# The border between an attention layer and its feed-forward layer: residual on TensorE, key sums ahead of the last X products, kv by rows of X, and the first tiles' outputs at other places

## The chip, the cores and the metric

The kernel runs on one core of one Trainium2 chip. The metric is the device time of one execution in microseconds (us). The kernel before took 1200.74, 1198.84 and 1199.76 us in three runs, 1199.76 in the median.

## The reference

Four residual layers over x of 2048 rows by 512 columns in bfloat16, and the gradient of the result with respect to x and all weights:

```python
phi = lambda t: jnp.where(t > 0, t + 1, jnp.exp(t)) + 1e-6
def _A_ref(x, wqkv, wo):                    # 32 heads of 16 columns
    q, k, v = split_heads(x @ wqkv)
    pq, pk = phi(q), phi(k)
    kv = einsum("bhsd,bhse->bhde", pk, v)
    z = einsum("bhsd->bhd", pk)
    o = einsum("bhqd,bhde->bhqe", pq, kv) / (einsum("bhqd,bhd->bhq", pq, z) + 1e-6)
    return merge_heads(o) @ wo
def _B_ref(x, w_gate, w_up, w_down):        # F = 1376
    return (sigmoid(x @ w_gate) * (x @ w_up)) @ w_down
x = x + _A_ref(layernorm(x), wqkv, wo)
x = x + _B_ref(layernorm(x), w_gate, w_up, w_down)
x = x + _A_ref(layernorm(x), wqkv, wo)
x = x + _B_ref(layernorm(x), w_gate, w_up, w_down)
```

The layers are called L0 (attention), L1 (feed-forward), L2 and L3; L0 and L2 share their weights, as L1 and L3 do.

## The kernel before, in words

The 2048 rows are 16 tiles (st = 0 to 15) of 128 rows. The order of each engine's instructions is that of the program text: it is written out by hand, and the engines run ahead of one another as far as the buffers allow. PSUM has eight banks in named pools: "t", "g" and "u" two banks each, "y" and "ln" one each (L144). A tile taken from a pool waits until the pool's oldest one has been read.

**Attention, first part (`kq_fwd`, L556).** For each tile the K and Q projections (L604), phi on ACT and DVE, and the running product X = pk-transposed times h, four accumulators of 128 by 512 in the "g" and "u" banks (L612). The value projection is never formed for every row: kv = X W_v. POOL adds the pk tiles up in `zs`, all but the last two. Then comes the part that the change rewrites, from L734 on: the sum over all rows, z, as products with matrices of ones: ones in float32 times `zs` (L735), then pk 14, the four X products of tile 14, pk 15 (L738); ACT copies z out as `zb` (L744). The four X products of tile 15 follow, each accumulator evacuated by ACT (L750), then kv from the four rows of X with the column block outermost (L758), masked on DVE to `kvbdT` (L760), M = kvbdT times wo (L765) in four banks, and MT (L776), which only the backward part reads. `late_q` does the Q projection of tiles 14 and 15, which was put off (L604 by its line); their `phi` halves finish it on DVE. A Sigmoid table is loaded on ACT (L771), as the feed-forward layer needs it.

**The attention outputs (`attn_fronts`, L805).** For one tile: `prod` is pq times zb on POOL, or on DVE (L815); `front1` sums it by head (DVE); `front2` adds epsilon, takes the reciprocal `rden` and scales pq to `pqn` (DVE, L831 to L833), and every second tile stores; `front3` transposes pqn on PE through the one "ln" bank (L355), and ACT copies it out as pqnT (L364); `attn_mm` is four products of pqnT with M into the "y" bank (L854); `attn_add` adds the old x on DVE (L862) and starts the layernorm statistics `ln.stats`: two DVE instructions (L448, L450) and three on POOL (L451 to L454), which leave `rstd` and `nmr`. `ln.apply` then normalizes on ACT (L459), and `stage_T` transposes h on PE through the "ln" bank, with DVE copying hT out.

**Feed-forward (`ab_fwd`, L892).** For each tile: gate and up products in three column blocks gu0, gu1, gu2 of 512, 512 and 352 columns (L909), two sigmoids on ACT (L911, L913), hh on DVE (L914), a product on POOL (L915), hh transposed in three groups `transposes(T, 0..2)` through the two "t" banks (L923) and copied out by ACT (L926, L928); `finish` is the down product of the tile before, into the "y" bank (L935), with its add on DVE (L937). The attention outputs of tile st + 2 or st + 3 are woven into tile st.

**Fill groups.** The weights' transposes for the backward part are cut into groups of four (some fewer) PE transposes through a "t" bank (L390 in L1, L416 and a like line in L3), with one evacuation on DVE or ACT. There are 16 groups in L1 and 34 in L3. Three are issued in `tail`, between `kq_fwd` and `ab_fwd`, a fourth at the end of tile 0; the rest are shared out by `fill.share(st)`, which is what is left over the tiles that are left: one for each of tiles 4 to 15 in L1, two for each of tiles 1 to 15 in L3. In a tile the first group goes behind gu0 and the others behind `finish` and `front3`, in front of `transposes(T, 2)`.

Of the kernel before, what the change touches and what calls it, by code (L numbers as in the profile page):

```python
# [67 lines left out]
def kernel(  # L68
# [78 lines left out]
    with tc.tile_pool(name="wfwd", bufs=1, reuse_waits="tile") as wfwd, ExitStack() as lctx, tc.manual_schedule(engines=EM):  # L147
# [44 lines left out]
        with tc.tile_pool(name="aq0", bufs=1, reuse_waits="tile") as aq:  # L192
            A = kq_fwd(k, aq, 0, lns[0], lns[1], x_bf)
            with tc.tile_pool(name="wt_stage", bufs=2, reuse_waits="tile") as wt_stage:
                fill = Fill(wT_groups_a(k, wt_stage))
                A.tail(fill)
                ab_fwd(k, A, lns[1], fill, nxt=lns[2])
        xctx.close()
        with tc.tile_pool(name="aq2", bufs=1, reuse_waits="tile") as aq:
# [32 lines left out]
            A.tail(fill)  # L232
# [229 lines left out]
class FwdLN:  # L462
# [9 lines left out]
    def stats(self, st):  # L472
        if st < NST:
            self.nmr[st] = ln_stats(self.k, self.k.xs[st][:], self.rstd(st))
# [13 lines left out]
    def stage_T(self, st):  # L488
        if st >= NST:
            return  # L490
        k = self.k
        h_t = self.hs.pop(st)
        hT = k.lnres["hT"].tile([P, NDC, P], BF16, name="hT")
        transpose_blocks(k, k.ps["ln"], hT[:], [h_t[:, c * P:(c + 1) * P] for c in range(NDC)], "vector", tag="ln_tp")
        self.hTs[st] = hT
# [60 lines left out]
def kq_fwd(k, aq, l, ln, ln_next, x_src=None):  # L556
# [10 lines left out]
    with ExitStack() as ctx:  # L567
# [7 lines left out]
        else:  # L575
            X_sb = big.tile([P, NDC, D], BF16, name="X_sb")
            MT_sb = big.tile([P, NDC, D], BF16, name="MT_sb")
        cnt = [0]
# [155 lines left out]
        z_ps = mm_tile()  # L734
        nc.tensor.matmul(z_ps[:], lhsT=k.ones32[:], rhs=zs, start=True, stop=False)  # L735

        def z_mm(st):
            nc.tensor.matmul(z_ps[:], lhsT=k.ones_sq[:], rhs=pk_all[:, st, :], start=False, stop=(st == NST - 1))  # L738

        for st in range(NST - ZLAG, NST - 1):  # L740
            z_mm(st)
        X_some(NST, NST - 2)
        z_mm(NST - 1)
# [3 lines left out]
        A.front2(0)  # L747
        for ic in range(NDC):
            X_mm(NST - 1, ic)
            nc.scalar.copy(X_sb[:, ic, :], X_ps[ic][:])  # L750
        nc.sync.dma_start(out=sv["X"].rearrange("(c p) j -> p c j", p=P), in_=X_sb[:])

        kv_ps = ps_tile(k, "y", [P, D], F32, "kv_ps")
        kv3 = kv_ps[:].rearrange("p (c f) -> p c f", c=NDC)
        for c in range(NDC):
            cs = slice(c * P, (c + 1) * P)
            for ic in range(NDC):
                nc.tensor.matmul(kv3[:, c, :], lhsT=k.wqkv[:, ic, 2 * D + c * P:2 * D + (c + 1) * P],  # L758
                                 rhs=X_sb[:, ic, cs], start=(ic == 0), stop=(ic == NDC - 1))
        nc.vector.tensor_tensor(kvbdT[:], kv3, k.bdmask[:].unsqueeze(1).to_broadcast([P, NDC, P]), ALU.mult)  # L760
        A.front3(0)
        A.prod(1, nc.vector)
        for c in range(NDC):
            m_ps = ps_tile(k, "gu"[c % 2], [P, D], F32, "M_ps")
            nc.tensor.matmul(m_ps[:], lhsT=kvbdT[:, c, :], rhs=k.wo[:, c, :], start=True, stop=True)  # L765
            evac_copy(k, A.M_sb[:, c, :], m_ps[:], "vector" if c % 2 else "scalar")
        A.front1(1)
        A.attn_y(0)
        A.front2(1)
        phis = [late_q(st) for st in range(NST - QLATE, NST)]  # L770
        nc.scalar.activation(k.tab[:], k.neg[:], ACT.Sigmoid)  # L771
# [6 lines left out]
        A.front3(1)  # L778
        phis[0]()
        A.ln.apply(0)  # L780
        for jc in range(NDC):
            nc.scalar.copy(MT_sb[:, jc, :], mt_ps[jc][:])
        nc.sync.dma_start(out=sv["MT"].rearrange("(c p) j -> p c j", p=P), in_=MT_sb[:])
        A.attn_mm(1)
        phis[1]()
    k.kv[l] = dict(kvbdT=kvbdT, zb=A.zb, rden_all=A.rden_all)

    def tail(fill):
        fill("tt", "vector")
        A.ln.stage_T(0)  # L790
        A.prod(2)
        A.prod(3)
        A.attn_add(1)
        A.front1(2)
        A.front2(2)
        A.extra = fill.mm("t")
    A.tail = tail
# [7 lines left out]
def attn_fronts(k, A, pool, small):  # L805
# [17 lines left out]
    def front2(st):  # L823
# [5 lines left out]
        den = f["den"]  # L829
        f["pqn"] = cur["pqn"][:, st % 2, :]  # L830
        nc.vector.tensor_scalar(den[:], den[:], EPS, None, ALU.add)  # L831
        nc.vector.reciprocal(A.rden_all[:, st, :], den[:])
# [6 lines left out]
    def front3(st):  # L839
        if st >= NST:  # L840
# [4 lines left out]
                         "scalar", tag="ln_tp")  # L845
        f["T"] = pqnT

    def attn_mm(st):
# [3 lines left out]
        y_ps = F_[st]["y"] = ps_tile(k, "y", [P, D], F32, "y_ps")  # L852
        for c in range(NDC):
            nc.tensor.matmul(y_ps[:], lhsT=pqnT[:, c, :], rhs=A.M_sb[:, c, :],  # L854
                             start=(c == 0), stop=(c == NDC - 1))
# [12 lines left out]

    A.attn_mm, A.attn_add = attn_mm, attn_add
    A.prod, A.front1, A.front2, A.front3, A.attn_y = prod, front1, front2, front3, attn_y  # L870


# [19 lines left out]
def ab_fwd(k, A, ln, fill, nxt=None, out_cb=None, last_cb=None):  # L892
# [3 lines left out]
    with ExitStack() as ctx:  # L896
# [53 lines left out]
        for st in range(NST):  # L950
# [5 lines left out]
            nfill = fill.share(st)  # L956
            if st == 0:
                gu(T, hT, 0)
                A.extra("vector")
                A.front1(FLAG)  # L960
                A.front3(2)
# [3 lines left out]
                A.attn_y(2)  # L965
                ln.stage_T(1)
                gu(T, hT, 2)
                A.front2(FLAG)
            else:
                A.prod(st + FLAG)  # L970
                gu(T, hT, 0)
                if st == 1:
                    A.front3(FLAG)
                else:
# [5 lines left out]
                if st == 1:  # L980
                    A.attn_y(FLAG)
# [3 lines left out]
                gu(T, hT, 2)  # L985
                A.front2(st + FLAG)
            if l == 1 and st == NST - 1:
                nc.scalar.activation(k.tab[:], k.neg[:], ACT.Exp)
            transposes(T, 1)
            ln.apply(st + YLAG)  # L990
# [5 lines left out]
            if st == 0:  # L996
                fill("t", "vector")
# [771 lines left out]
```

## Time and profile before

| | |
|---|---|
| three runs | 1200.74, 1198.84, 1199.76 us; median 1199.76 |
| the profiled execution | 1199.19 us |
| its span | 1197.5 us (1.69 lie around it) |
| mean granted TensorE clock | 0.998 |

Busy time of one engine over the span counts its instructions' durations, a matmul's from its start to its last result. Where the share of PE is high, what matters is when it stands still. For that the region of the change is cut into stretches, which are the same for both pairs of layers: from the z sum (L735) to the first gate product of tile 0 (L909), from there to the first of tile 1, and from there to the first product of finish(0) (L935).

| stretch | L0 to L1 (us) | L2 to L3 (us) |
|---|---|---|
| z to tile 0's first gate product | 53.57 to 70.49 | 260.26 to 276.08 |
| to tile 1's | 70.49 to 79.80 | 276.08 to 285.38 |
| to finish(0) | 79.80 to 86.20 | 285.38 to 292.01 |

The column PEclk of a stretch is the clock that the throttle granted: 1.00 is full speed, and it falls to 0.50 in whole windows of 3.41 us.

### The profile page before, as it was taken

What the parts mean: (1) busy time and instruction counts of PE and PEld (TensorE: products, weight loads), DVE (VectorE), ACT (ScalarE), POOL (GpSimd) and SP (SyncE); (2) the same over time, 40 slices, a digit from 0 to 9 for tenths busy, and PEclk for the clock granted to TensorE, in tenths of its full rate; (3) what the DMA queues carried; (4) which work ended last, traced back from release to release, by engine and by line L of the source; (5) the groups of instructions that cost most, each with busy time, mean ns of one, the idle gap of its engine ahead of it and who ended that gap; (6) DMA issues with size and microseconds to landing.
All of it is one profiled execution on the core that took longest, in us unless ns stands there. A gap on an engine that the chain in (4) does not pass through costs nothing.

```text
span 1197.5 us, 21853 instructions
## 1 busy us (share of the span) xinstructions
PE 1175.6 (98%) x8302; PEld 717.0 (60%) x8302; DVE 730.5 (61%) x1414; ACT 593.2 (50%) x1100; POOL 290.2 (24%) x498
## 2 busy tenths in 40 slices
PE   8989999998999999999999999999999999999999
PEld 4445555544555555555556568965556745547888
DVE  7788886777777556665784760056664976761211
ACT  6667776546776754543644651144444635630010
POOL 5646765425666410000110010000100110110000
PEclk9999999999999999999999999999999999999999
DMA  8834455434446777976856859558897685749875
GB/s 269 291 124 164 169 177 186 155 137 166 179 152 220 248 224 249 333 228 208 260 177 200 251 162 314 141 157 260 257 296 223 219 262 169 220 127 338 280 199 163
DMA packets 266233, 256.05 MB, mean 214 GB/s; under 512 B 43280, under 2 KB 251024, under 8 KB 261264
## 3 DMA queue, kind: packets, MB, share of 16 engines
q1 hardware_dynamic: 266128, 254.65, 66.6%
q8 instruction: 65, 1.06, 0.4%
q14 instruction: 40, 0.33, 0.1%
HBM read 135.69 MB, written 118.92 MB: 213 GB/s over the span
## 4 chain that ended last, share of the span: by engine, by line
PE 93%; DVE 4%; ACT 2%; DMA 1%; issue 0%; POOL 0%; DVEq 0%; ACTq 0%
PE p_ps L1412 17%; PE dh_ps L1174 13%; PE dh_ps L1627 7%; PE p_ps L1396 6%; PE dhh_ps L1059 6%; PE u_ps L909 6%; PE g_ps L909 6%; PE y_ps L935 6%; PE T_ps L1134 3%; PE y_ps L854 2%; PE GT_ps L1539 2%; PE dpk_ps L1658 2%; PE dp_ps L1514 2%; PE t_mm L604 2%; PE t_tp L923 2%; PE X_ps L612 2%
## 5 line engine op out<-in xcount | busy, mean ns | idle before, releaser
L1412 PE MATMUL p_ps<-p_set,p_a 128*128 128x256 bf16 (+1 forms) x2032 | 210.3, 264 | 0.4 <-DVE dw_stg L1386 0.4
L1412 PEld LDWEIGHTS <-p_a 128*128 128x128 bf16 x2048 | 186.0, 98 | 22.8 <-issue 0.5
L1067 DVE TENSOR_TENSOR dd<-dhh_ps,ssd 128x512 bf16<-128x512 f32 x144 | 82.5, 629 | 134.3 <-PE dhh_ps L1059 131.3
L1138 ACT COPY ddT<-T_ps 128x1024 bf16<-128x1024 bf16 (+1 forms) x96 | 83.0, 867 | 124.7 <-PE T_ps L1134 124.3
L1033 POOL TENSOR_SCALAR ab<-c 128x2 f32<-128x2 f32 x64 | 12.3, 191 | 435.7 <-DVE junk L1030 421.5
L915 POOL TENSOR_TENSOR ssd_t<-hh_t,oms 128x512 bf16<-128x512 bf16 (+1 forms) x96 | 101.6, 1064 | 55.5 <-ACT out_t L219 41.1
L1174 PEld LDWEIGHTS <-ddT 128*128 128x128 bf16 (+1 forms) x704 | 67.7, 98 | 69.3
L909 PEld LDWEIGHTS <-hT 128*128 128x128 bf16 x768 | 71.1, 98 | 56.6 <-DVE hT L362 1.0
L1386 DVE TENSOR_TENSOR dw_stg<-p_ps,dw_stg 128x512 bf16<-128x512 f32 (+3 forms) x43 | 28.0, 653 | 106.7 <-PE p_ps L1412 84.9
L909 PE MATMUL g_ps<-wg,hT 128*128 128x512 bf16 (+1 forms) x384 | 90.0, 357 | 0.6 <-DVE hT L362 0.6
L909 PE MATMUL u_ps<-wu,hT 128*128 128x512 bf16 (+1 forms) x384 | 90.0, 357 | 0.0
L914 DVE TENSOR_TENSOR hh_t<-u_ps,ssd_t 128x512 bf16<-128x512 f32 (+1 forms) x96 | 61.0, 636 | 45.9 <-PE u_ps L909 24.5
L1174 PE MATMUL dh_ps<-wgT,ddT 128*128 128x512 bf16 (+1 forms) x352 | 86.2, 379 | 0.0
L1059 PE MATMUL dhh_ps<-wdT,gT 128*128 128x512 bf16 x372 | 82.5, 357 | 0.0
L935 PE MATMUL y_ps<-wd,hhT 128*128 128x512 bf16 (+1 forms) x352 | 81.3, 379 | 0.6 <-DVE x L937 0.6
L1174 PE MATMUL dh_ps<-wuT,ddT 128*128 128x512 bf16 (+1 forms) x352 | 81.3, 379 | 0.0
L1396 PE MATMUL p_ps<-p_a,p_set 128*128 128x512 bf16 (+1 forms) x352 | 81.2, 379 | 0.0
L1025 ACT ACTIVATE t_sb<-dh_ps,rstd_all 128x512 f32<-128x512 f32 x64 | 44.0, 687 | 72.1 <-issue 38.4
L1030 DVE SCALAR_TENSOR_TENSOR junk<-t_sb,h_ld 128x512 bf16<-128x512 f32 x64 | 44.0, 687 | 49.3 <-ACT t_sb L1025 48.4
L911 ACT ACTIVATE ssd_t<-g_ps 128x512 bf16<-128x512 f32 (+1 forms) x96 | 53.2, 554 | 30.8 <-PE g_ps L909 30.6
L1388 ACT CAST dw_stg<-p_ps 128x512 bf16<-128x512 f32 (+2 forms) x43 | 24.1, 560 | 65.9 <-PE p_ps L1412 58.9
L1396 PEld LDWEIGHTS <-p_set 128*128 128x128 bf16 (+1 forms) x352 | 33.6, 100 | 34.9
(241 smaller groups left out, 2164.4 us busy)
## 6 DMA issues: line engine op xcount, KB each, us to landing
p_set<-sv_hdd SPq DMA_DIRECT2D x30, 1024.0 KB, 6.0
sv_ssd<-ssd_t SPq DMA_DIRECT2D x32, 688.0 KB, 3.4
ssd<-sv_ssd SPq DMA_DIRECT2D x24, 688.0 KB, 5.1
sv_hdd<-dd SPq DMA_DIRECT2D x48, 320.0 KB, 3.6
sv_hdd<-hh_t SPq DMA_DIRECT2D x32, 320.0 KB, 2.6
h_ld<-sv_h SPq DMA_DIRECT2D x32, 256.0 KB, 4.6
p_a<-sv_h SPq DMA_DIRECT2D x16, 512.0 KB, 6.1
p_set<-sv_dqk SPq DMA_DIRECT2D x8, 1024.0 KB, 7.8
```

The costliest lines, as they stand in the source:

```text
L909: nc.tensor.matmul(ps[:, 0:w], lhsT=hT[:, kc, :], rhs=w_sb[:, kc, c0:c0 + w], start=(kc == 0), stop=(kc == NDC - 1))
L911: nc.scalar.activation(ssd_t[:, 0, c0:c0 + w], g_ps[:, 0:w], ACT.Sigmoid)
L914: nc.vector.tensor_tensor(hh_t[:, c0:c0 + w], u_ps[:, 0:w], ssd_t[:, 0, c0:c0 + w], ALU.mult)
L915: nc.gpsimd.tensor_tensor(ssd_t[:, 1, c0:c0 + w], hh_t[:, c0:c0 + w], oms[:, 0:w], ALU.mult)
L935: nc.tensor.matmul(y_ps[:], lhsT=T["hhT"][0:r, fc, :], rhs=k.wd[0:r, fc, :], start=(fc == 0), stop=(fc == NFC - 1))
L1059: k.nc.tensor.matmul(ps[:, 0:w], lhsT=gT[:, jc, :], rhs=k.wdT[:, jc, c0:c0 + w], start=(jc == 0), stop=(jc == NDC - 1))
L1067: k.nc.vector.tensor_tensor(dd[:, a, c0:c0 + w], ps[:, 0:w], ssd[:, a, c0:c0 + w], ALU.mult)
L1138: nc.scalar.copy(ddT[:, :, f0:f0 + nfull, :], tps[:, :, 0:nfull, :])
L1174: nc.tensor.matmul(T["dh"][:], lhsT=ddT_block(T, a, fc), rhs=(k.wuT, k.wgT)[a][0:r, fc, :], start=(i == 0), stop=(i == 2 * NFC - 1))
L1396: nc.tensor.matmul(ps[0:r, :], lhsT=set_t[:, st, c * P:c * P + r], rhs=self.ops[j["l"], "g"][:, st, :], start=(st == 0), stop=(st == NST - 1))
L1412: nc.tensor.matmul(ps[:, icl * w:(icl + 1) * w], lhsT=self.ops[j["l"], "h"][:, st, ic * P:(ic + 1) * P], rhs=set_t[:, st, 0:w], start=(st ...
L1627: nc.tensor.matmul(dh_ps[:], lhsT=lhsT, rhs=rhs, start=(i == 0), stop=(i == len(ops) - 1))
```

## The change

- z: the ones products for `zs`, pk 14 and pk 15 are issued in a row into the "y" bank, in front of the X products that are left.
- X: the fourth accumulator is evacuated by DVE instead of ACT.
- kv: the row of X is the outer loop and the column block the inner one, in a "t" bank; behind rows 0 and 1 stands one more product each (`on(1)`: identity times pk of tile 0, 128x512, whose result nobody reads). `rden(0)` is split off `front2(0)`, and the latter stands behind the mask.
- Tiles 0 and 1: `attn_res` adds the old x on PE as the first product into the "y" bank, the identity times x: in bfloat16 in L0 (the input x), in float32 in L2 (a float32 identity `eye32`, made on POOL with the pools). `attn_out` then takes the statistics from PSUM, and ACT copies x out of PSUM behind them. `attn_add(1)` is gone from the tail.
- In L0 alone: `on(2)` behind the first residual product and `keep_on()(3)` behind the second, five more such products.
- late_q(14) stands in front of attn_mm(0), late_q(15) behind the MT products; the copies of MT are issued one by one between other ACT work; the pqnT of tile 1 is evacuated by DVE, hT of tile 0 by ACT; the Sigmoid table load comes last.
- `tail` is gone, and so is the fourth group at the end of tile 0: all fill groups fall into `share`, which gives one for each of tiles 1 to 14 and two for tile 15 in L1, two for each of tiles 1 to 11 and three for each of tiles 12 to 15 in L3.
- Tile 0: attn_y(2) moves from in front of gu2 to behind transposes(1), and front3(2) behind gu2. Tile 1: front3(3) stands behind gu1, attn_y(3) behind gu2.

The backward part is untouched. The diff, cut to its core:

```diff
+        if l == 0:
+            eye = k.ident
+        else:
+            eye = big.tile([P, P], F32, name="eye32")
...
-        z_ps = mm_tile()
+        z_ps = ps_tile(k, "y", [P, D], F32, "z_ps")
         nc.tensor.matmul(z_ps[:], lhsT=k.ones32[:], rhs=zs, start=True, stop=False)
+        for st in range(NST - ZLAG, NST):
             nc.tensor.matmul(z_ps[:], lhsT=k.ones_sq[:], rhs=pk_all[:, st, :], start=False, stop=(st == NST - 1))
-        for st in range(NST - ZLAG, NST - 1):
-            z_mm(st)
-        X_some(NST, NST - 2)
-        z_mm(NST - 1)
         nc.scalar.copy(A.zb[:], z_ps[:])
         A.prod(0, nc.vector)
         A.front1(0)
-        A.front2(0)
+        X_some(NST, NST - 2)
         for ic in range(NDC):
             X_mm(NST - 1, ic)
-            nc.scalar.copy(X_sb[:, ic, :], X_ps[ic][:])
+            evac_copy(k, X_sb[:, ic, :], X_ps[ic][:], "vector" if ic == NDC - 1 else "scalar")
+        A.rden(0)
+        on = keep_on()
+        kv_ps = ps_tile(k, "t", [P, D], F32, "kv_ps")
+        for ic in range(NDC):
+            for c in range(NDC):
...
+            if ic < NDC - 2:
+                on(1)
+        nc.vector.tensor_tensor(kvbdT[:], kv3, ...)
+        A.front2(0, False)
+        A.attn_res(0, eye)
+        if l == 0:
+            on(2)
...
         A.front3(0)
+        phis = [late_q(NST - 2)]
+        A.attn_mm(0)
         A.prod(1, nc.vector)
+        A.attn_out(0)
+        A.prod(2)
         A.front1(1)
-        A.attn_y(0)
         A.front2(1)
...
+        mt_copy(0)
+        mt_copy(1)
+        phis.append(late_q(NST - 1))
+        A.ln.apply(0)
+        A.attn_res(1, eye)
+        if l == 0:
+            keep_on()(3)
+        A.front3(1, "vector")
+        mt_copy(2)
+        A.ln.stage_T(0, "scalar")
         phis[0]()
+        A.attn_mm(1)
+        mt_copy(3)
+        A.attn_out(1)
         phis[1]()
+        nc.scalar.activation(k.tab[:], k.neg[:], ACT.Sigmoid)
...
-    def tail(fill):
-        fill("tt", "vector")
-        A.ln.stage_T(0)
-        A.prod(2)
-        A.prod(3)
-        A.attn_add(1)
-        A.front1(2)
-        A.front2(2)
-        A.extra = fill.mm("t")
...
+    def attn_res(st, ident):
+        y_ps = F_[st]["y"] = ps_tile(k, "y", [P, D], F32, "y_ps")
+        nc.tensor.matmul(y_ps[:], lhsT=ident[:], rhs=k.xs[st][:] if A.x_src is None else A.x_src[:, st, :],
+                         start=True, stop=False)
+
+    def attn_out(st):
+        y_ps = F_.pop(st)["y"]
+        A.ln.stats(st, y_ps[:])
+        nc.scalar.copy(k.xs[st][:], y_ps[:])
...
+            A.prod(st + FLAG)
             if st == 0:
+                A.front1(2)
                 gu(T, hT, 0)
-                A.extra("vector")
-                A.front1(FLAG)
-                A.front3(2)
+                A.front2(2)
                 ln.apply(1)
                 gu(T, hT, 1)
                 transposes(T, 0)
-                A.attn_y(2)
                 ln.stage_T(1)
                 gu(T, hT, 2)
-                A.front2(FLAG)
+                A.front3(2)
             else:
-                A.prod(st + FLAG)
                 gu(T, hT, 0)
-                if st == 1:
-                    A.front3(FLAG)
-                else:
+                if st > 1:
                     A.attn_y(st + YLAG)
...
                 gu(T, hT, 1)
                 if st == 1:
-                    A.attn_y(FLAG)
+                    A.front3(FLAG)
                 transposes(T, 0)
                 ln.stage_T(st + 1)
                 A.front1(st + FLAG)
                 gu(T, hT, 2)
+                if st == 1:
+                    A.attn_y(FLAG)
                 A.front2(st + FLAG)
...
             transposes(T, 1)
+            if st == 0:
+                A.attn_y(2)
+                A.front1(FLAG)
+                A.front2(FLAG)
             ln.apply(st + YLAG)
-            if st == 0:
-                fill("t", "vector")
```

## Prediction

> **What bounds the kernel now.** I read the page first: PE's share, then the chain.
>
> ```profile
> span 1197.5 us, 21853 instructions
> ...
> PE 1175.6 (98%) x8302; PEld 717.0 (60%) x8302; DVE 730.5 (61%) x1414; ACT 593.2 (50%) x1100; POOL 290.2 (24%) x498
> ...
> PE 93%; DVE 4%; ACT 2%; DMA 1%; issue 0%; POOL 0%; DVEq 0%; ACTq 0%
> ```
>
> PE is the bound, and the chain leaves it for DVE and ACT 6% of the time. PE work that is moved costs what it cost; only PE's idle time can be won. So I split the region that the diff touches, at both borders (L0 into L1, L2 into L3), into three stages: from the z sum to the first gate product of the first tile (st0), on to that of st1, on to the first product of finish(0). This is the view of busy time by stretches:
>
> ```profile
> core 0: us, PE busy (x) PEld busy (x) DVE busy (x) ACT busy (x) POOL busy (x), PEclk, DMA share, GB/s
> 56.43:59.84 3.41, 2.08 (x22) 1.26 (x20) 2.73 (x6) 2.21 (x6) 0.00 (x0) 1.00 0.46 162
> 59.84:63.26 3.42, 3.06 (x8) 1.14 (x9) 2.46 (x5) 1.59 (x3) 0.00 (x0) 0.50 0.32 111
> 271.47:274.88 3.41, 2.02 (x22) 1.21 (x20) 2.83 (x5) 3.38 (x7) 3.07 (x4) 1.00 0.43 150
> 53.57:70.49 16.92, 13.44 (x89) 6.89 (x88) 12.72 (x27) 10.01 (x18) 3.43 (x5) 0.90 0.40 142
> 260.26:276.08 15.82, 12.30 (x88) 6.41 (x87) 12.09 (x26) 9.85 (x18) 3.43 (x5) 1.00 0.33 114
> 276.08:285.38 9.30, 7.15 (x51) 3.96 (x52) 7.85 (x18) 5.38 (x11) 4.15 (x7) 1.00 0.18 63
> 285.38:292.01 6.63, 6.63 (x51) 3.86 (x50) 4.58 (x10) 4.97 (x11) 5.00 (x5) 1.00 0.70 234
> ```
>
> A stage's busy PE counts each matmul's latency. By issue pitch (bf16 128x512 0.216 us, 128x352 0.149, 128x128 0.056; f32 128x512 0.86, the two records of the ones32 row, .43 apart, being one product) L2's stages hold 10.40, 6.79 and 6.63 us of work, so 5.42, 2.51 and 0 us of idle. L0's later stages read 9.31 and 6.40. L0's first is 1.10 longer than L2's: in 59.84 to 63.26 the granted clock is 0.50 and eight 512-wide products stand 0.42 apart. In the window ahead, PE's starts fill 0.37 of the time.
>
> **Step 1, z to g_ps.** The sums of the last two pk tiles move in front of eight X products: zb starts at 261.8 instead of 262.6. The X copies were four on ACT (2.06 us, paced by ACT); the fourth now goes to DVE. With kv by rows of X, three rows run as their copies land and only the last waits: kv ends 1.02 earlier, and so do kvbdT and M (266.88 to 265.86). Added on PE: L2 two f32 identity products (1.72) and two fillers (0.43); L0 two bf16 ones and seven fillers (1.94). The f32 product was never run here as an identity: bound 0.22 (bf16 row) to 0.86 (ones32 row), taken 0.86, the same type and shape. The first lies under the wait for kvbdT (264.9 to 265.8); uncovered, either costs 0.86.
>
> late_q(14)'s four products (0.86) now stand in the wait for M's copies, their exp on ACT behind two of these. On POOL, L2's two instructions for eye32 come with the pools at the head of the layer, some 40 us ahead of their use (its first projections are at 219.1), and on SP the MT store goes behind attn_mm(1); nothing in the forward pass reads it.
>
> Then y(0) at 267.9, BN 269.0 (from PSUM, unseen: between 0.42, a DVE copy out of PSUM, and 0.81, ACT's apply of this shape; taken 0.69, its own row from SBUF below), apply at 271.3. Transposes of pqn(1) start at 271.86; stage_T(0) needs the one "ln" bank, which DVE's evacuation (0.39) frees at 272.76; hT(0) goes by ACT (0.58): 272.76 + 0.17 + 0.26 + 0.58 + 0.07 = 273.85 is the new g_ps. Stage: 13.59 against 15.82. Its work is 10.40 + 2.15 − 0.67 (three fill groups gone, step 4) = 11.9, so its idle falls from 5.42 to 1.7.
>
> **Step 2, st0.** ACT has the x copy of tile 1 (0.58; up to 0.81 by the apply row) and the Sigmoid table load (1.28 in its row) in front of sig0, now 276.5. PE waits 0.64 for hh, 0.27 at stage_T(1), 0.35 at front3(2), and 0.62 for pqnT(2). attn_y(2) runs at 281.27, behind transposes(1) instead of in front of gu2. Next g_ps: 282.30. Stage 8.45 against 9.30: 6.79 − 0.22 (one group gone) of work and 1.88 of idle.
>
> **Step 3, st1: what attn_y(2)'s new place costs.** The trace has the same chain, under other work:
>
> ```profile
> 281.71 1.03 PE L854 MATMUL y_ps<-M_sb,pqnT 128*128 128x512 bf16 x4
> ...
> 282.77 0.69 DVE L862 TENSOR_TENSOR x<-y_ps,x 128x512 f32<-128x512 f32 x1 [0.31 <-PE y_ps L854]
> ...
> 283.50 0.69 DVE L448 BATCH_NORM_STATS2 ln_stats<-x 128x6 f32<-128x512 f32 x1
> ...
> 284.23 0.18 DVE L450 BATCH_NORM_AGGREGATE ln_mv<-ln_stats 128x2 f32<-128x6 f32 x1
> ...
> 285.48 0.27 POOL L454 TENSOR_SCALAR ln_nmr<-ln_mv,rstd_all 128x1 f32<-128x1 f32 x1
> ...
> 285.78 0.81 ACT L459 ACTIVATE hstage<-x,ln_nmr,rstd_all 128x512 bf16<-128x512 f32 x1 [0.78 <-POOL ln_nmr L454]
> ...
> 286.90 0.59 ACT L911 ACTIVATE ssd_t<-g_ps 128x512 bf16<-128x512 f32 x1
> ```
>
> From the add to the apply it is 3.0 us, and the apply stands in ACT's queue in front of the hhT copies and the next sig0. After: y(2)'s last product 281.9, add 282.3, apply 285.35. ACT stands 3.66, and sig0, whose g_ps is ready at 283.2, comes at 286.5; hh 287.1, t_tp(0) 287.88. PE idles 1.67 there, 1.05 at stage_T(2) (the "ln" bank waits for pqnT(3)'s copy behind them on ACT) and 0.73 at finish(0) (the "y" bank waits for tile 3's add). Stage 10.08 against 6.63.
>
> L2: 13.59 + 8.45 + 10.08 = 32.12 against 31.75, **+0.37**. L0 at full clock likewise 32.12 against 32.63: **−0.51**. At each border a wait of 0.38 in st2 (front3(4) behind pqnstage; 89.12 in L0) goes with the shift: **−0.75**.
>
> **Step 4, the fill groups.** Four transposes cost 0.22. Four per border lay in idle time; all now fall into the full loop: in L1 three are paid (0.67), in L3 four (0.89). L1's last tile gets two, its 512 KB store then standing in SP's queue in front of the next layer's hT: 0.27, bounds 0 to 1.7. L3's tiles 12 to 15 get three instead of two. The "t" ring has two banks, taken in the order fill1, t0, t1, fill2, fill3, t2: t2's transposes wait for fill2's evacuation, on DVE behind finish's add or on ACT. The trace has such a ring wait at the old tail:
>
> ```profile
> 274.52 0.61 PE L416 MATMUL wT_ps<-ident,wd 128*128 128x128 bf16 x8
> ...
> 274.94 0.76 DVE L362 COPY wdT<-wT_ps 128x512 bf16<-128x512 bf16 x2 [0.57 <-PE wT_ps L416]
> ...
> 275.42 0.32 PE L416 MATMUL wT_ps<-ident,wd 128*128 128x128 bf16 x3
> ```
>
> The eight were issued by 274.96, the next at 275.42: 0.46 idle. With the add in front I get 0.65, 0.62, 0.87, 0.62: **+2.76**.
>
> **Step 5, the clock.** Step 3's waits (1.67, 0.22 of work, 1.05) make a 3.41 us stretch with PE's share down to 0.20, and one that starts anywhere within about 2.0 of 3.41 us falls below 0.43, the share that kept full clock from 271.47; 0.37 lost it. So each border probably has one half-clock window. Price: 1.1 (L0's row) to 1.7 (half of 3.41), taken 1.4. One, **+1.4**; L0's old one is already left out above.
>
> The Trainium skill, "TensorE: Matmul & The Clock Gate", section "Why this matters for your kernels", asks for no PE-idle gap above about 3 us, one such window bringing half clock; by it 1.67 is harmless, which is rival B. Here the window at half clock followed gaps of 0.46 us at most, so the trace disagrees. The page's section "A second HAM failure mode: psum-queue depth-cycling", frequent micro-idles, is what the trace shows.
>
> **Sum** on the profiled execution, 1199.19 (span 1197.5 and 1.69 around it; 0.57 below the median 1199.76): −0.51 + 0.37 − 0.75 + 0.67 + 0.89 + 0.27 + 2.76 = +3.70, 1202.9; with one slow window **1204.3**. With two 1205.7, up to 1206.3 at 1.7 each.
>
> **Rivals.**
> - **A, forecast, 0.56**: own range 1202.9 to 1206.3.
> - **B, full clock at both borders, 0.16**: 1202.9. For it: 271.47 held at 0.43. Against: 0.37 did not, and 0.20 is lower.
> - **C, third fills hidden, 0.09**: where ACT takes the extra evacuations (every other tile) they land in time, half of 2.76 goes, and the clock holds too: 1204.3 − 1.38 − 1.4 = 1201.5. For: ACT is 50% busy. Against: 0.46 at the tail though DVE came at once.
> - **D, the other side, 0.12**: step 3's chain doesn't hold PE. sig0 would have to run as soon as g_ps is ready (283.2), so that nmr(2) follows y(2) by under 1.2 us instead of 3.4; then both borders lose 3.45 of idle and the slow window goes: 1204.3 − 6.9 − 1.4 = 1196.0. For: before has the chain and no idle at all in that stage. Against: the 3.0 us above, and ACT's order.
> - **E, the fillers don't do what they say, 0.07**: L0 keeps its slow window: 1204.3 + 1.1 = 1205.4.
>
> Two in ten left out are D and the ends of A: **1201.0 to 1206.5**; the unknown f32, BN and copy costs (each under 0.9, partly covered) lie within it. A measurement tells some 0.2%, 2.4 us, from no change (1197.4 to 1202.2): faster is D, 0.12; C and the low end of B, 0.12, are the same; slower 0.76.
>
> **What would show it.** Right: M 1.0 earlier after z; stages near 13.6, 8.45, 10.1; ACT idle over 3 us ahead of apply(2); t2's transposes waiting in L3's tiles 12 to 15; a granted clock of 0.5 just behind st1's start. Wrong: stage 3 near 6.6 (D), clock 1.00 throughout (B), no idle in those four tiles (C), 0.5 within L0's first stage (E). The forecast fails most easily on step 3, which gives 6.9 of the sum's terms, and on the clock, whose windows shift from run to run.

## The result and the profile after

The changed kernel takes 1206.11 us in the median (1205.15 to 1207.33, 6 runs), the kernel before, on the same chip, 1200.05 (1198.84 to 1200.74, 6 runs): a ratio of 1.0051, 95% interval 1.0039 to 1.0064. It is slower by some 6 us, inside the range of 1201.0 to 1206.5 and 1.8 above the forecast of 1204.3. The profiled execution took 1206.06 with a span of 1204.3.

The page of the changed kernel, its span, its busy times and the chain by engine:

```profile
span 1204.3 us, 21892 instructions
...
PE 1179.6 (98%) x8317; PEld 718.6 (60%) x8317; DVE 728.1 (60%) x1409; ACT 595.4 (49%) x1105; POOL 291.7 (24%) x500
...
PE 64%; DMA 1%; DVE 0%; ACT 0%; issue 0%; DVEq 0%
```

PE is busy 4.0 us longer, about what the added products take by issue pitch (1.94 in L0 and 2.15 in L2), and the rest of the 6.8 us of span is PE standing still. (The chain names PE 64% here: it was followed back less far, which says nothing of the time.) The busy time by stretches, cut at the same marks as before, L0 first, then L2:

```profile
core 0: us, PE busy (x) PEld busy (x) DVE busy (x) ACT busy (x) POOL busy (x), PEclk, DMA share, GB/s
54.03:68.16 14.13, 12.76 (x86) 6.31 (x85) 10.54 (x22) 8.21 (x16) 2.63 (x4) 1.00 0.44 153
68.16:77.32 9.16, 7.25 (x48) 3.72 (x48) 6.20 (x12) 7.40 (x14) 5.29 (x7) 1.00 0.32 109
77.32:87.29 9.97, 7.13 (x51) 3.91 (x50) 7.27 (x15) 5.47 (x12) 5.75 (x7) 1.00 0.30 112
262.87:276.43 13.56, 12.72 (x83) 6.35 (x82) 10.10 (x21) 8.21 (x16) 2.63 (x4) 1.00 0.28 98
276.43:285.60 9.17, 7.26 (x49) 3.73 (x49) 6.17 (x12) 7.40 (x14) 5.28 (x7) 1.00 0.44 139
285.60:295.56 9.96, 7.12 (x51) 3.90 (x50) 7.27 (x15) 5.47 (x12) 5.75 (x7) 1.00 0.52 183
```

The first stage is the one that the change shortens, the third pays it back, and PEclk is 1.00 in all six. The whole way from L0's z to the backward part's first product (L1059 before, L1092 after) goes from 371.15 to 377.21 us:

| stretch | before | after | difference | forecast |
|---|---|---|---|---|
| L0: z to finish(0) of L1 | 32.63 | 33.26 | +0.63 | −0.51 |
| finish(0) of L1 to L2's z | 174.06 | 175.58 | +1.52 | −0.37 + 0.67 + 0.27 = +0.57 |
| L2: z to finish(0) of L3 | 31.75 | 32.70 | +0.95 | +0.37 |
| finish(0) of L3 to the backward part | 132.71 | 135.67 | +2.96 | −0.37 + 0.89 + 2.76 = +3.28 |
| half-clock windows opened by the change | | 0 | 0 | +1.4 |
| ahead of L0's z and behind the start of the backward part | | | +0.46, +0.28 | 0 |

The 32.63 of before holds its own half-clock window (1.1). The last row lies outside what was changed. L0's z comes between 53.3 and 56.0 us in the twelve traces of this study, so below kernels are compared by the stretches of their traces and by the medians of their runs, and a difference of the medians under about 1 us is not leaned on. One of e3's five executions took 1765.46 us at a mean granted clock of 0.654 and is left out of e3's figures.

### The profile page after: what moved, and what is told of

Read it like the earlier page. It is cut to its first block, busy times and chain, and to the rows that moved or that the text cites. A ratio compares the mean times of both kernels' runs of the same rounds, so it can differ in the third digit from the quotient of the medians.

```text
span 1204.3 us, 21892 instructions
## 1 busy us (share of the span) xinstructions
PE 1179.6 (98%) x8317; PEld 718.6 (60%) x8317; DVE 728.1 (60%) x1409; ACT 595.4 (49%) x1105; POOL 291.7 (24%) x500
## 4 chain that ended last, share of the span: by engine, by line
PE 64%; DMA 1%; DVE 0%; ACT 0%; issue 0%; DVEq 0%
PE p_ps L1445 17%; PE dh_ps L1207 13%; PE dh_ps L1660 7%; PE p_ps L1429 6%; PE dhh_ps L1092 6%; PE T_ps L1167 3%; PE GT_ps L1572 2%; PE dpk_ps L1691 2%; PE dp_ps L1547 2%; PE T_ps L1687 1%; PE t_ps L353 1%; PE gT_ps L1512 1%; PE gT_ps L1084 1%; DMA out_dram<-dw_stg 1%; PE y_ps L968 0%; PE fin_ps L1739 0%
## 5 line engine op out<-in xcount | busy, mean ns | idle before, releaser
L1092 PE MATMUL dhh_ps<-wdT,gT 128*128 128x512 bf16 x372 | 82.5, 357 | 0.0
L944 ACT ACTIVATE ssd_t<-g_ps 128x512 bf16<-128x512 f32 (+1 forms) x96 | 53.3, 555 | 27.8 <-PE g_ps L942 27.6
L968 PEld LDWEIGHTS <-hhT 128*128 128x128 bf16 (+1 forms) x352 | 33.2, 98 | 36.1 <-issue 1.9
```

Of the source, the lines that this page charges most:

```text
L944: nc.scalar.activation(ssd_t[:, 0, c0:c0 + w], g_ps[:, 0:w], ACT.Sigmoid)
L968: nc.tensor.matmul(y_ps[:], lhsT=T["hhT"][0:r, fc, :], rhs=k.wd[0:r, fc, :], start=(fc == 0), stop=(fc == NFC - 1))
L1092: k.nc.tensor.matmul(ps[:, 0:w], lhsT=gT[:, jc, :], rhs=k.wdT[:, jc, c0:c0 + w], start=(jc == 0), stop=(jc == NDC - 1))
```

## The experiments

All but e8 and e10 change the changed kernel; e8 and e10 change the kernel before. Each was timed in 4 to 11 runs beside the kernel before on one chip, whose medians there were 1198.57, 1199.71 and 1199.09 us in the three groups (e1 to e4, e5 to e8, e9 and e10).

### e1: the apply of tile 2 later on ACT

```diff
                 gu(T, hT, 0)
-                if st > 1:
+                if st == 1:
+                    ln.apply(2)
+                else:
                     A.attn_y(st + YLAG)
...
-            ln.apply(st + YLAG)
+            if st > 0:
+                ln.apply(st + YLAG)
```

> The changed kernel with one ACT instruction moved: the layernorm apply of tile 2 goes from the end of st0 to behind the two sigmoids of st1's gu0, at both borders. Theory (the apply, waiting for nmr, holds the sigmoids and copies behind it on ACT): stage 3 falls from 9.97 to about 8.6 us per border, since the wait in front of t_tp (1.65) goes and stage_T(2) still waits for the later hT; 2.9 us in all, 1203.2. Rival 1 (the statistics chain itself is what PE waits for, wherever the apply stands): no change, 1206.1. Rival 2 (nothing but the apply's place holds PE): stage 3 back at 6.6, 1199.3.

Measured: 1203.06 us, ratio 1.0034 (1.0021 to 1.0046), against 1.0051 for the changed kernel. Stage 3 is 8.56 in L0 and 8.57 in L2, the others keep 14.13, 9.16 and 13.57, 9.16. ACT's timeline in the changed kernel:

```profile
80.37 0.81 ACT L457 ACTIVATE hstage<-x,ln_nmr,rstd_all 128x512 bf16<-128x512 f32 x1 [3.65 <-POOL ln_nmr L452]
...
81.50 0.60 ACT L944 ACTIVATE ssd_t<-g_ps 128x512 bf16<-128x512 f32 x1
```

and with the apply behind the sigmoids:

```profile
79.16 0.60 ACT L944 ACTIVATE ssd_t<-g_ps 128x512 bf16<-128x512 f32 x1 [0.33 <-PE g_ps L942]
...
81.13 0.81 ACT L457 ACTIVATE hstage<-x,ln_nmr,rstd_all 128x512 bf16<-128x512 f32 x1 [0.89 <-POOL ln_nmr L452]
```

ACT stood 3.65 us for nmr with a sigmoid behind it whose input was ready; now the sigmoid runs first and the wait is 0.89. So the theory holds with its size: the place in ACT's queue costs 1.4 us a border. Rival 1 is out. Rival 2 (all 3.4 us) is out too: 1.93 us of idle stay in L2, 0.32 in front of t_tp, 0.89 at stage_T(2), where the next hT needs that apply at whatever place it stands, and 0.72 at the "y" bank.

### e2: attn_y(2) back in front of gu2

```diff
                 gu(T, hT, 1)
+                A.front3(2)
                 transposes(T, 0)
+                A.attn_y(2)
                 ln.stage_T(1)
                 gu(T, hT, 2)
-                A.front3(2)
...
             if st == 0:
-                A.attn_y(2)
                 A.front1(FLAG)
```

> The changed kernel with attn_y(2) put back in front of st0's gu2 and front3(2) in front of transposes(0), at both borders. Theory (the first tiles run ahead of the attention outputs, so a wait is only moved): stage 2 rises by about 1.7, stage 3 falls by about 2.1, 0.8 us less in all, 1205.3. Rival (the new place of attn_y(2) is itself what costs): stage 3 back at 6.6 to 7 with stage 2 unchanged at 9.2, 6 to 7 us less, 1199.5.

Measured: stage 2 10.89 (+1.72), stage 3 7.96 (−2.01) at both borders, 0.7 us less from z to the backward part (376.47). The times: 1205.64 and 1206.12 in the two runs with the full clock, 1207.05 to 1208.33 in the three whose mean granted clock is 0.996 or 0.997; ratio 1.0066 (1.0053 to 1.0079). The theory holds by the trace: with the shorter first stage the products of tile 0 meet an attention output that is not ready, and its place decides only in which stage PE waits. The place alone, which the forecast's step 3 blamed, is worth 0.3 us a border.

### e3: fill groups in tiles 0 and 1

```diff
                 gu(T, hT, 1)
+                if True:
+                    fill("t", "vector")
                 transposes(T, 0)
...
                 if st == 1:
                     A.front3(FLAG)
+                    if True:
+                        fill("tt", "vector")
                 transposes(T, 0)
+                if st == 1 and True:
+                    fill("t", "vector")
```

> The changed kernel with four fill groups at each border again: one in st0 in front of transposes(0), two in st1 in front of transposes(0) and one behind it; so no tile of L3 has three and L1's last tile has one. Theory (three groups in a tile wait for the ring of two t banks, and the second group of L1's last tile delays the next layer's first hT): the four waits of 0.6 to 0.8 in L3 and the 1.3 and 0.3 at the start of L2 go (4.3), 1.5 us of transposes leave the loops, about 2 come back in stages 2 and 3; 3.9 less, 1202.2. Rival 1 (the waits in L3 are those of another engine): they stay, 1205. Rival 2 (the groups cost in st1 what they cost in the loop): 1206.

Measured: from finish(0) to L2's z 173.64 (−1.94 against the changed kernel), from L3's finish(0) to the backward part 132.16 (−3.51): the waits of both loops go with the third group and with the second one of L1's last tile, and rival 1 is out. The stages give back 0.33 each in st0. In st1 this trace has a half-clock window at each border, in 85.49 to 88.90 and 293.70 to 297.11, and stage 3 reads 12.28 and 12.04; with 1.66 taken off for the window, as e4, e6 and e7 measure it below, the groups cost an estimated 0.65 and 0.41 there. With the 0.33 that is about the issue time of four groups (0.89), so it is the waits that stay away, and rival 2, by which nothing would be won, is out: the run with clock 1.0 took 1203.0, those with 0.999 and 0.997 1204.2 and 1205.3 to 1206.0. Ratio 1.0047 (1.0034 to 1.0061). So most of what was expected comes, and in some executions a window of half clock takes it back.

What the waits in L3 look like in the changed kernel, at the end of tile 12 (DVE and PE in turn, in order of time):

```profile
401.50 0.69 DVE L970 TENSOR_TENSOR x<-y_ps,x 128x512 f32<-128x512 f32 x1 [0.46 <-PE y_ps L968]
401.52 0.61 PE L431 MATMUL wT_ps<-ident,wg 128*128 128x128 bf16 x8
402.10 0.75 DVE L360 COPY wgT<-wT_ps 128x512 bf16<-128x512 bf16 x2
402.57 0.33 PE L956 MATMUL t_tp<-ident,hh_t 128*128 128x128 bf16 x3 [0.44 <-DVE wgT L360]
```

Two groups are issued in a row; their evacuations stand behind finish's add on DVE; and transposes(T, 2) starts when the first of them has freed its bank. By issue pitch PE idles 0.60, 0.61, 0.83 and 0.61 in the four tiles.

### e4: the woT store behind the last tile's stores

```diff
-                            nc.sync.dma_start(
+                            st_dma = lambda: nc.sync.dma_start(
...
+                            if w_sb is k.wo:
+                                k.late_store = st_dma
+                            else:
+                                st_dma()
...
             nc.sync.dma_start(out=sv["hdl"][0, :, st, :], in_=T["hh"][:, NG * GW:F])
+            if l == 1 and st == NST - 1:
+                k.late_store()
```

> The changed kernel with one DMA issue moved: the 512 KB store of woT is issued behind the three stores of L1's last tile instead of in front of the last of them; the second group stays. Theory (the buffer of L2's first hTst waits for the store of hh, which stands behind woT's on the queue): the waits of 1.30 and 0.34 at the start of L2 go, 1204.6. Rival (the second fill group itself, its transposes and its copy on ACT, delays the start of L2): no change, 1206.1.

Measured: from finish(0) to L2's z 174.23 (−1.35). In the changed kernel, SP's queue, DVE and PE:

```profile
217.77 0.37 SPq L393 DMA_DIRECT2D woT_d<-wt_st  x1
218.19 0.80 SPq L1041 DMA_DIRECT2D sv_hdl<-hh_t  x1
...
223.59 0.69 DVE L360 COPY hTst<-hT_tp 128x1024 bf16<-128x1024 bf16 x1 [1.70 <-DMA sv_hdl<-hh_t]
...
225.26 1.02 PE L609 MATMUL t_mm<-wqkv,hTst 128*128 128x512 bf16 x4 [1.14 <-DVE pk_all L632]
```

The copy into hTst may not begin before the store of hh has read its buffer; the store landed 5.20 us after its issue, behind woT's 512 KB. In e4 hh's store landed 3.48 us after its issue at 216.08 and the copy ran at 221.10 without a wait. Two delays are gone together: SP issued hh's store 1.78 us after that of ssd in the changed kernel, because woT's store stands ahead of it in SP's queue and waits for its copy on ACT, and 0.45 after it in e4; and the landing took 1.72 less. So the cause is woT's store ahead of hh's; the second group's transposes and copy stayed, and the rival is out. The time did not show it (1206.62, ratio 1.0066, 1.0053 to 1.008): no run had the full clock, and the profiled one has a half-clock window of its own, the third of these rows:

```profile
283.93:287.34 3.41, 3.41 (x22) 1.67 (x21) 3.01 (x7) 0.76 (x2) 1.85 (x4) 1.00 0.55 215
287.34:290.75 3.41, 1.14 (x15) 0.79 (x13) 1.71 (x4) 3.37 (x9) 2.37 (x3) 1.00 0.78 246
290.75:294.17 3.42, 3.42 (x12) 1.47 (x10) 1.50 (x3) 0.82 (x2) 1.27 (x2) 0.50 0.11 42
```

(The row ahead of it, with PE busy 1.14 of 3.41, is the reason, see e10.) It makes L2's stage 3 11.64 instead of 9.97: one window costs 1.67 us. The expectation left this out.

### e5: rden(2) in front of hh0

```diff
                 A.front1(2)
+                A.rden(2)
                 gu(T, hT, 0)
-                A.front2(2)
+                A.front2(2, False)
```

> The changed kernel with the two small DVE instructions of rden(2) in front of st0's hh0, where DVE waits anyway, so that pqn(2) follows hh0 at once and starts ahead of POOL's product of hh0. In the changed kernel's trace pqn(2) takes 1.32 us, lying under that product, and 0.69 in other places. Theory (of the two instructions the one that comes second stands until the first is done): pqn(2) takes 0.69 and ends 1.1 earlier, POOL's product takes 1.7 instead of 1.15; the wait of 0.87 at front3(2) goes, attn_y(2) comes some 0.6 earlier, stage 2 is 8.5 instead of 9.17 and the whole 1.2 less, 1204.9. Rival (pqn(2) is long there for another reason): still 1.32, 0.5 earlier, at most 0.9 less in all, POOL unchanged.

Measured: stage 2 is 8.45 at both borders, where 9.17 stood. The two instructions in the changed kernel:

```profile
72.54 1.15 POOL L948 TENSOR_TENSOR ssd_t<-hh_t,oms 128x512 bf16<-128x512 bf16 x1 [0.74 <-ACT oms L946]
...
72.91 1.32 DVE L852 TENSOR_TENSOR pqnstage<-pq_all,rden_all 128x512 bf16<-128x512 bf16 x1
```

and with DVE first:

```profile
74.10 0.68 DVE L852 TENSOR_TENSOR pqnstage<-pq_all,rden_all 128x512 bf16<-128x512 bf16 x1
...
74.31 1.48 POOL L948 TENSOR_TENSOR ssd_t<-hh_t,oms 128x512 bf16<-128x512 bf16 x1 [1.10 <-ACT hstage L457]
```

The one that comes second pays: DVE 0.64 (1.32 to 0.68) or POOL 0.33 (1.15 to 1.48, where 1.7 was expected). The theory holds. The Trainium skill, "SBUF — State Buffer", section "Who interferes with whom", says that a DVE instruction with two SBUF inputs contends with a GpSimd one that reads SBUF, and that the order of issue decides who blocks; these rows agree. The whole is 1205.74 (ratio 1.0055, 1.0043 to 1.0068), 1205.5 to 1205.7 in the runs near full clock and 1207.3 in the two at 0.997: from z to the backward part it is 1.9 us less, of which 1.4 is the two borders' stage 2 and 0.5 a wait in L0's z sum that is not there in this trace. The whole hardly shows it, since L0's z itself comes 1.9 later here (55.95).

### e6: no filler products

```diff
-            if ic < NDC - 2:
-                on(1)
...
-        if l == 0:
-            on(2)
...
-        if l == 0:
-            keep_on()(3)
```

> The changed kernel without the nine filler products: seven in L0 (two between the rows of kv, two and three behind the residual products), two in L2; nobody reads their result. Theory (they lie in idle time and only keep the granted clock up): the three stages keep their lengths (14.1, 9.2, 10.0 in L0) where the clock is full, but a window of half clock falls into L0's first stage in some executions, 1.1 to 1.7 us each; median 1206.1 to 1207.5. Rival (the clock holds without them, and they cost PE time): no window there and stage 1 shorter by up to 0.4 us, 1205.5.

Measured: 1206.80 (ratio 1.006, 1.0047 to 1.0074). The stages are 14.13, 9.17, 9.97 and 13.56, 9.16, so the fillers cost nothing, as the theory has it; but no half-clock window falls into the first stage. In a trace, half-clock windows lie whole multiples of 3.41 us apart (208.21 us in e3, 61 windows; 17.06 in e7, 5 windows), as on a grid that is laid anew in every execution. Shifting this grid over e6's trace, the emptiest window of the first stages still has PE's products in 0.45 of it. The profiled run has its window in L2's stage 3 (291.90, stage 11.61). So what the theory said of the clock in stage 1 is wrong: with the residual on PE and the new order there the fillers are not needed. The start of L2 shows no wait of 1.30 in this run: hh's store landed 3.87 us after its issue instead of 5.20. The DMA packets of the traces tell the two apart. One load of instructions, a packet of 16 KB, runs from 220.68 to 221.61 in the changed kernel, in the midst of the two stores, and the last packet of hh's store ends at 222.84; in e6 the load starts at 222.47, just as that store ends. In all five traces in which it falls into the stores (the changed kernel, e1, e2, e5, e7) hh's store lands after 5.1 to 5.2 us and hTst waits for it; in e6 neither happens. No run moved the load, so that it causes the delay is argued, not tested.

### e7: the residual on DVE

```diff
-        A.attn_res(0, eye)
...
-        A.attn_out(0)
+        A.attn_add(0)
...
-        A.attn_res(1, eye)
...
-        A.attn_out(1)
+        A.attn_add(1)
```

> The changed kernel with the residual of tiles 0 and 1 added on DVE again, as in the kernel before (no identity product, no ACT copy out of PSUM, statistics from SBUF). Theory (the product lies in idle time, and the add and its hop are on the chain to hT(0)): stage 1 is 0.7 longer per border, 14.3 in L2, 1.5 in all, 1207.6. Rival 1 (the float32 identity product costs its 0.86 in the open): L2's stage 1 does not grow, 1206.1 or less. Rival 2 (the ACT copies it brings hold the sigmoids): stage 2 falls by 0.6 and pays for it, 1206.3.

Measured: 1210.17 (ratio 1.0087, 1.0074 to 1.0101). L0's stage 1 is 14.85, 0.72 longer; stage 2 9.10, 0.06 shorter; L2's 14.61 is 1.05 longer, but its last 0.67 us lie in a half-clock window, which can take up to 0.33 of that. So the residual on PE is worth 0.7 us a border, and both rivals are out. The other 2.6 us are clock: all four runs read 0.994 to 0.997, and the trace has two windows in L2 alone (278.33 and 295.39).

### e8 and e10: the head alone, and with fillers

e8 puts the change's z sums, the fourth X copy on DVE, kv by rows of X and front2(0) behind the mask into the kernel before. e10 adds ten filler products to it:

```diff
             if ic < NDC - 2:
+                on(1)
...
+        on(8)
         nc.vector.tensor_tensor(kvbdT[:], kv3, ...)
```

> The kernel before with the head of the change alone: z sums in front of the last X products, the fourth X row on DVE, kv by rows of X (no fillers between), front2(0) behind the mask; residual, tail, fill groups and the places of the outputs as before. Theory (M is 1.0 earlier but front2(0), now behind kvbdT, makes y(0) wait for pqn(0) and DVE's queue): M 1.0 earlier, the first gate product no earlier or up to 0.4 later, within 0.5 us of the kernel before at full clock per border. Rival (the head's gain arrives): stage 1 is 14.8 instead of 15.8 in L2, 2 us less in all.

> The head of the change on the kernel before, as in the run without fillers, plus ten filler products: one each behind kv rows 0 and 1, eight in front of front3(0), where PE idles 2.15 us. In the ten traces so far a window of half clock follows every window of 3.41 us in which PE's products fill 0.37 or less of the time (nine of nine) and none in which they fill 0.38 or more. Theory (PE's share in the grid's window decides): the fillers lift the share above 0.5, all runs have the full clock, stage 1 is 16.1 us in L2 and 16.2 to 16.7 in L0, about 1.5 us per border less than without them: 1199.7 against 1202.7. Rival (something else in that stretch lowers the clock, or the fillers cost PE time): 1202 or more.

Measured: e8 1202.69 (ratio 1.0028, 1.0018 to 1.0038), e10 1200.10 (1.0005, 0.9996 to 1.0014). Of e8's expectation M comes later, not earlier: PE waits 2.15 us for pqn(0), with M behind front3(0) in its queue.

```profile
266.57 0.69 DVE L756 TENSOR_TENSOR kvbdT<-kv_ps,bdmask 128x512 bf16<-128x512 f32 x1 [0.92 <-PE kv_ps L753]
...
267.77 0.69 DVE L830 TENSOR_TENSOR pqnstage<-pq_all,rden_all 128x512 bf16<-128x512 bf16 x1
...
268.51 0.40 PE L355 MATMUL ln_tp<-ident,pqnstage 128*128 128x128 bf16 x4 [1.99 <-DVE pqnstage L830]
268.75 1.53 PE L762 MATMUL M_ps<-wo,kvbdT 128*128 128x512 bf16 x4
```

kvbdT is ready at 267.3, and M, 1.5 later, is the first to use it. The changed kernel puts M in front of front3(0), and this order, not the early kv alone, brings its M forward. At the full clock (e10) L2's stage 1 is 16.27 and L0's 16.82, no shorter than the 15.83 of before.

e8 reads 17.66 and 17.43, with a half-clock window at each border (60.92 and 269.13); in e10 the eight fillers lie in the same idle time, and all 11 runs have the full clock: some 2.6 us for work that nobody reads (the medians of before in the two groups are 0.6 apart). The theory holds and the rival is out; the stages are a little longer than expected. Why is told by the grid. Of the twelve traces, PE's products fill the nine windows ahead of a half-clock one to 0.23, 0.23, 0.24, 0.28, 0.29, 0.29, 0.31, 0.33 and 0.37 of their time (counted by issue pitch, with the doubled pitch at half clock); of all the other windows from L0 to the end of L3 none is under 0.38. The lowest and the highest of the nine, and the two lowest of the others:

| trace | window (us) | PE's share | next window's clock |
|---|---|---|---|
| e7 | 291.98 | 0.23 | 0.50 |
| before | 56.43 | 0.37 | 0.50 |
| e5 | 288.40 | 0.38 | 1.00 |
| e2 | 73.97 | 0.43 | 1.00 |

### e9: all together

The edit rewrites both tiles; this is what it changes in their order. Above the mark is st0, below it st1.

```diff
                 A.front1(2)
+                A.rden(2)
                 gu(T, hT, 0)
-                A.front2(2)
+                A.front2(2, False)
                 ln.apply(1)
                 gu(T, hT, 1)
+                fill("t", "vector")
                 transposes(T, 0)
...
                 gu(T, hT, 0)
+                ln.apply(2)
                 fill("t", "vector")
                 gu(T, hT, 1)
                 A.front3(3)
+                fill("tt", "vector")
                 transposes(T, 0)
+                A.attn_y(3)
+                fill("t", "vector")
                 ln.stage_T(2)
                 A.front1(4)
                 gu(T, hT, 2)
-                A.attn_y(3)
```

> The changed kernel with what the earlier runs point to, all within tiles 0 and 1 of the feed-forward layers: rden(2) in front of hh0; the apply of tile 2 behind gu0's sigmoids; four to six fill groups again in tiles 0 and 1 (one in front of st0's transposes(0), one behind st1's gu0, two in front of and one behind its transposes(0)); attn_y(3) in front of gu2 in st1 so that finish(0) finds the y bank free. Theory (each wait found goes, and the fill groups lie in what is left): stages 13.6, 8.7, 8.7 us, no third group in L3, no wait at the start of L2, and no stretch with PE idle enough to lose the clock; 1198.1, level with or up to 1 us below the kernel before at full clock (1198.5). Rival (the groups in st1 take DVE from the chain and open new waits): stage 3 stays near 10, 1201.

Measured: 1197.79 (1197.26 to 1198.02, 11 runs), ratio 0.9988, interval 0.9979 to 0.9996: 1.3 us below the kernel before and some 8 below the changed one. L2's three stages:

```profile
259.47:273.04 13.57, 12.68 (x81) 6.34 (x82) 10.12 (x21) 8.20 (x16) 2.63 (x4) 1.00 0.28 98
273.04:281.78 8.74, 7.08 (x51) 4.02 (x52) 6.64 (x13) 7.41 (x14) 5.58 (x7) 1.00 0.44 143
281.78:290.13 8.35, 7.55 (x63) 4.51 (x61) 7.07 (x16) 5.08 (x11) 4.86 (x6) 1.00 0.66 220
```

They add up to 30.66 against 31.75 before and 32.70 after, with five fill groups in them, as before, and one in the changed kernel; from L3's finish(0) on it is 133.04, against 132.71 and 135.67. All 11 runs have the full clock: by the grid shifted over the trace, no window of the borders is below 0.58. The rival is out.

## Why the prediction was right, and where its steps were not

The forecast (slower, 1204.3) and the range held. The mechanism it named was there; one term of the sum did not come, and others came that it had at less.

- **What bounds it:** right. The borders' idle time and the loops' fill groups make 6.1 of the 6.8 us of span.
- **Step 1:** right in L2, 13.56 against 13.59, with 1.6 of idle where 1.7 stood. In L0 it failed: 14.13. The step took L0 to be like L2. But pk 15's product now stands directly behind pk 14's instead of four X products (0.86) later, and in L0 DVE has pk 15 ready only at 55.6:

```profile
54.89 0.38 PE L747 MATMUL z_ps<-pk_all,ones_sq 128*128 128x512 bf16 x1
55.61 0.38 PE L747 MATMUL z_ps<-pk_all,ones_sq 128*128 128x512 bf16 x1 [0.34 <-DVE pk_all L632]
```

  That is 0.50 by issue pitch, a cover that was taken away and not priced. The instructions that the trace of before did not have cost what was taken: the statistics from PSUM 0.698 (0.69), the copy of x out of PSUM 0.586 (0.58), and the float32 identity product has records of 0.592, as the ones32 product has; the first of them hides under the wait for kvbdT.
- **Step 2:** too small, 8.45 against 9.17. Of its four waits two came as forecast, 0.23 at stage_T(1) and 0.62 for pqnT(2). The one at front3(2) was 0.87 where 0.35 stood: pqn(2) takes 1.32 here and 0.69 in tile 2 of before, where POOL's product does not run beside it. In tiles 4 to 15 of before that product does, and pqn takes 0.89 to 1.04, so the price could have been read there. The wait for hh was 0.85 where 0.64 stood: ACT's copy of x waits 0.52 for the statistics, in front of the table load and sig0. With DVE first (e5) the stage is 8.45; that this is the forecast's number is chance, as the wait for hh is 1.14 there.
- **Step 3:** right, 10.08 against 9.97: waits of 1.65, 0.96 and 0.72 where 1.67, 1.05 and 0.73 stood, and ACT idle 3.65 in front of the apply. What it blamed was half right. Of the 3.4 us, the apply's place in ACT's queue is 1.4 (e1) and the place of attn_y(2) almost nothing (e2): it moves 1.7 of them into stage 2. The rest is tile 2's output coming no earlier while tile 0 does: in L2 attn_mm(2) starts 21.45 us after z before and 21.68 after, and tile 0's first gate product comes 2.27 earlier. That these 2 us follow from it is argued from the times; no run tested it alone.
- **Step 4, L3:** right. The four waits of transposes(T, 2) add up to 2.65 (forecast 2.76), on the instructions that it named. The row it leaned on was misread, though: between the two rows of wT_ps four transposes of stage_T(0) run, at 274.96, so PE idled 0.23 there and not 0.46.
- **Step 4, L1's last tile:** the mechanism was nearly right, woT's store standing in SP's queue, but in front of hh's store, for whose buffer hTst waits (e4). The size was not: 0.27 was taken from bounds of 0 to 1.7, and 1.70 came (from the finish of tile 14 to L2's z: 46.82 before, 48.52 after); the wait for hh's store is 1.30 and 0.34 of it. On the other hand the rest of L1 is 0.18 shorter, where +0.30 was forecast: a second wait, 0.30 at 107.32, went with the first, which is 0.54 by issue pitch where the prediction took 0.38.
- **Step 5, the clock:** did not come. Five of the six runs have the full clock; the sixth, 1207.33, reads 0.999, which one window would give; no trace shows where it lay. The threshold was right in kind: between 0.37 and 0.49 by the trace of before, between 0.37 and 0.38 by all. (The prediction's 0.43 for the window from 271.47 leaves out the end of the MT products, 0.23 us of work; with them it is 0.49.) The price was a little low, 1.4 against 1.64 to 1.68. What failed is "probably": over the changed kernel's own trace the grid falls below 0.375 in 0.46 of its positions at either border, not in 2.0 of 3.41; and the sum then counted one window, although its text gave each border one. L1's and L3's finish(0) are 208.27 us apart, 61.0 windows, so both borders meet the grid almost alike, and mostly both would lose a window or neither. In the profiled execution the emptiest stretch lay across two windows, and both kept 0.58 or more.

So of the rivals it was B, full clock at both borders, and its price of 1202.9 was 3.2 below the profiled 1206.06: 0.5 in L0's z, 1.4 in the two stages 2, 1.4 at the start of L2, 0.7 at the ends of the trace, less 1.0 in terms that were set too high. That these and the slow window that stayed away (1.4) left only 1.8 between them is chance. Rivals C and D are out (four waits measured; stage 3 near 10), and E: e6 shows that in this order L0's first stage keeps its clock without fillers. The rule of the Trainium skill that the prediction cites ("TensorE: Matmul & The Clock Gate", section "Why this matters for your kernels") asks for no gap above about 3 us, and it is not what decides here: the trace disagrees, as e3 lost the clock with PE busy 1.42 of 3.41 us, its idle time split over several gaps, the longest 1.33.

```profile
82.08:85.49 3.41, 1.42 (x18) 1.10 (x18) 2.32 (x5) 2.84 (x8) 2.37 (x3) 1.00 0.22 77
85.49:88.90 3.41, 3.41 (x16) 1.74 (x14) 1.91 (x4) 1.18 (x3) 0.40 (x1) 0.50 0.46 158
```

**Where the gain went.** Stage 1 did lose 2.27 us in L2, 0.7 of it by the residual on PE. It was given back in stage 3, because nothing had brought tile 2's output forward; and the fill groups, which had lain free in the idle time, went into loops that had none. Their waits, more than their work, cost 4.3 us.

## What to carry to other kernels

Work that lies in idle time is free only there: before it is moved out, count the buffers (a ring of two banks) and the queue in front of the next stage at its new place, not only its instructions. When one tile is brought forward, find the next late one, and see which engine would stand at it with ready work queued behind. Where an engine's clock depends on how full it is, compare the emptiest window that a fixed grid could catch, not the longest gap.

## What the runs showed of the hardware

- From L0 to the end of L3, in all twelve traces, the granted clock halves for one window of 3.41 us exactly when PE's products filled 0.37 or less of the window ahead (nine of nine, and no window at 0.38 or more); such a window costs 1.64 to 1.68 us where PE is the bound (e4, e6, e7), and some ten products of 0.216 us, whose results nobody reads, prevent it (e10).
- DVE's pqn and POOL's products of 352 or 512 columns hold each other up: pqn took 0.69 without one, 0.90, 1.03, 1.20 and 1.32 with 0.35, 0.49, 0.65 and 0.78 us of POOL's product left at its start, which is that rest and 0.55. A tiny DVE instruction is held as well: in e5 the 128x32 add of rden(2), 0.18 alone, took 0.92 behind POOL's prod.
- hh's store behind woT's landed 5.1 to 5.2 us after its issue in the five traces in which a 16 KB load of instructions ran within the two stores, and 3.87 us after it in the one in which the load came later (e6); that 1.3 us opened or closed a wait of 1.30 us on PE.
